# Attention and two MLPs on one core: q and k of three batches in blocks of 32 tokens, transposed by VectorE, and another order of the attention pieces

## The chip, the core and the metric

The kernel runs on one core of a Trainium2 chip. A core has TensorE (matrix products; PE in the rows, and PEld for its weight loads), VectorE (DVE), ScalarE (ACT), GpSimd (POOL), and SyncE (SP), whose queue issues most of the transfers between the chip's memory and the core's on-chip memory (SBUF). Matrix products are written to PSUM. The metric is the time of one execution in microseconds (us); lower is better.

## The reference

There are 4 batches, 8 heads, 576 tokens and 64 dimensions a head. Attention is the sum of two parts: a local one, in which a token looks at the tokens less than 4 away, and a downsampled one, in which q, k and v are averaged over groups of 4 tokens, attended to in full (144 x 144), and the result repeated 4 times. The result, 2304 tokens of 512 numbers, goes through two MLPs.

```python
q_d = q.reshape(B, H, Sd, factor, D).mean(axis=3)      # k_d, v_d alike
out_up = np.repeat(sm_attn(q_d, k_d, v_d), factor, axis=2)
mask = np.abs(pos[:, None] - pos[None, :]) < factor
scores = np.where(mask, scale * np.matmul(q, k.transpose(0, 1, 3, 2)), -1000000000.0)
# softmax, times v, plus out_up; then with x of shape (2304, 512):
h = x @ w_in;  g = h * (1.0 / (1.0 + np.exp(-1.702 * h)));  x = g @ w_out
h = x @ w_in2; g = np.where(h > 0.0, h, np.exp(np.minimum(h, 0.0)) - 1.0); y = g @ w_out2
```

## The kernel before

Attention is worked in units of one batch and two heads. Batch 0 is cut in two, four `early` units (token windows 0 to 3) and four `late` ones (windows 4 to 8), so that the first MLP can begin; the other three batches are the twelve units of `rest`. A window is 64 tokens of q against 70 of k. A unit is a list of pieces, in `pieces` (L560): the front transposes q and k (`trans`, L400: three transposes by TensorE into PSUM, a copy into `qT` or `kT` by ScalarE at L410, and after a tensor's second piece a sum over groups of four by VectorE, L416), makes the local scores (`qk`, L421: products, mask and maximum), the downsampled scores (`qk_down`, L452), and in the last piece the exponents and normalization (`exps`, L471). The back transposes the probabilities (`pdt`, `pt`) and multiplies with v (`pv_down`, `pv`). A whole unit has 8 pieces in front and 8 behind. `load_qk` (L345) brings q and k of a unit in by four transfers, six neighbouring tokens to a partition; the next unit's load is issued in the piece `k1` (L568), behind the last transposes.

The loop at L614 writes one queue: the first four front pieces of a unit, then back pieces of the unit before in turn with the rest of the front. `attend` (L639) gives out the next piece; a piece that ends a unit is held back while its block of tokens has no free buffer (L644).

The first MLP goes over the tokens in six blocks (two of 256, three of 512, one of 256), and over the hidden features in steps. A step is the products into the hidden layer (`h`, L676), their activation (ScalarE L686, VectorE L689, with a split of each number in two parts, L690 and L691), and two steps later the products out of it (`y`, L711). The loop at L903 sets all this in order: each chunk of products, half a step's `h` or half its `y`, is followed by one attention piece (three of them in the first steps), and before a block begins its attention is finished (L906). The blocks 0 and 1 are taken in turn, and during them the 32 weight tiles of the first MLP are converted by ScalarE and VectorE (`conv_w`, L144: tiles `wst1`, `ww1`, `whl1`), one part after each chunk. The hidden products have two PSUM buffers, and from that loop on all attention pieces share two (`spool`). The second MLP (`h`, L823, `o`, L872) follows, with its own weights loaded in the last block of the first.

What an engine does is in order: each has one list of instructions, made by a scheduler from the order of the code, and waits there for what an instruction needs.

Of the kernel before, what the change touches and what calls it, by code (L numbers as in the profile page):

```python
# [16 lines left out]
ALU = mybir.AluOpType  # L17
AX = mybir.AxisListType

P = 128  # L20
D = 64
S = 576
SD = 144
HALF = 72
NWIN = 9
# [41 lines left out]
def kernel(  # L67
# [20 lines left out]
    nc = tc.nc  # L88
# [16 lines left out]
    mask = cpool.tile([P, 6, KW], BF16, tag="mask", name="mask")  # L105
    nc.gpsimd.memset(mask, 0.0)
    for half in range(2):
        rows = slice(64 * half, 64 * half + 64)
        for a, e, lo in ((0, 1, -3), (1, 5, 0), (5, 6, 3)):
            m = mask[rows, a:e, :]  # L110
            for step, base, mult in ((1, -lo, -1), (-1, lo + 6, 1)):
                nc.gpsimd.affine_select(
                    out=m, in_=m, pattern=[[0, e - a], [step, KW]], compare_op=ALU.is_ge, fill=NEG,
# [193 lines left out]
    class Unit:  # L307
# [37 lines left out]
        def load_qk(self):  # L345
            self.raw = []
            b, hp = self.b, self.hp
            for nm, src in (("q", q), ("k", k)):
                r = self.t([96, 6, 2, D], f"raw{nm}")
                for j in range(2):  # L350
                    nc.sync.dma_start(
                        out=r[:, :, j, :], in_=src[b, 2 * hp + j].rearrange("(p t) d -> p t d", t=6)
                    )
                self.raw.append(r)
# [45 lines left out]
        def trans(self, which, i):  # L400
            raw = self.raw[which]
            if i == 0:
                self.qkT[which] = self.t([P, S], ("qT", "kT")[which])
            pt = self.ps([P, 3, 96], f"pt{which}{i}")
            for j in range(3):
                nc.tensor.transpose(  # L406
                    out=pt[:, j, :], in_=raw[:, 3 * i + j].rearrange("p h d -> p (h d)"),
                    identity=ident[:96, :96],
                )
            nc.scalar.activation(  # L410
                out=self.qkT[which].rearrange("c (p t) -> c t p", t=6)[:, 3 * i:3 * i + 3, :],
                in_=pt, func=AF.Copy, scale=(0.125, 1.0)[which],
            )
            if i == 1 and self.dn_from is None:
                d = self.t([P, SD], ("qd", "kd")[which])
                nc.vector.tensor_reduce(  # L416
                    out=d, in_=self.qkT[which].rearrange("c (g r) -> c g r", r=4), axis=AX.X, op=ALU.add
                )
                self.qkd[which] = d

        def qk(self, a, e):  # L421
            if a == self.w0:
                self.sl = self.t([P, self.nwin, KW], "sl", bufs=2)
                self.nm = self.t([P, NWIN], "nm", bufs=4)
            ps = self.ps([P, e - a, KW], f"qk{a}")
            m0 = 0 if a == 0 else 6 - (e - a) if e == NWIN else 1
            by_pe = self in early or self in late
            if by_pe:
                nc.tensor.matmul(
                    out=ps.rearrange("p a b -> p (a b)"), lhsT=identb,  # L430
                    rhs=mask[:, m0:m0 + e - a].rearrange("p a b -> p (a b)"),
                    start=True, stop=False, skip_group_check=True,
                )
            for w in range(a, e):
                ks = win_start(w)
                for j in range(2):
                    r = slice(64 * j, 64 * j + 64)
                    nc.tensor.matmul(  # L438
                        out=ps[r, w - a, :], lhsT=self.qkT[0][r, 64 * w:64 * w + 64],
                        rhs=self.qkT[1][r, ks:ks + KW], start=not by_pe, stop=True, skip_group_check=True,  # L440
                    )
            if by_pe:
                for w in range(a, e):
                    self.scores[w] = ps[:, w - a, :]
                scores = ps
            else:
                scores = self.sl[:, a:e]
                nc.vector.tensor_tensor(out=scores, in0=ps, in1=mask[:, m0:m0 + e - a], op=ALU.add)
            nm = self.nm[:, a:e]
            nc.vector.tensor_reduce(out=nm, in_=scores, axis=AX.X, op=ALU.max, negate=True)  # L450

        def qk_down(self, j):  # L452
            if j == 0:
                self.nmd = self.t([HALF, 4], "nmd", bufs=4)
                self.pd = self.t([HALF, 4, SD], "pd")
                self.psd = []
            r = slice(64 * j, 64 * j + 64)
            ps = self.ps([HALF, 2, SD], f"qkd{j}")
            for c in range(2):
                nc.tensor.matmul(  # L460
                    out=ps[:, c, :], lhsT=self.qkd[0][r, c * HALF:(c + 1) * HALF], rhs=self.qkd[1][r, :],
                    start=True, stop=True,
                )
            nc.vector.tensor_reduce(
                out=self.nmd[:, 2 * j:2 * j + 2], in_=ps, axis=AX.X, op=ALU.max, negate=True
            )
            if j == 1:
                nc.vector.tensor_scalar(out=self.nmd, in0=self.nmd, scalar1=1 / 16, scalar2=None, op0=ALU.mult)
            self.psd.append(ps)

        def exps(self):  # L471

# [2 lines left out]
            if down:  # L475
                for i in range(4):
                    nc.scalar.activation(
                        out=self.pd[:, i, :], in_=self.psd[i // 2][:, i % 2, :], func=AF.Exp,
                        bias=self.nmd[:, i:i + 1], scale=1 / 16, accum_out=sums[:HALF, NWIN + i:NWIN + i + 1],
                    )  # L480
            for w in range(self.w0, self.w1):
                nc.scalar.activation(
# [77 lines left out]
        def pieces(self):  # L560
# [1 line left out]
            down = self.dn_from is None  # L562
            nxt = following.get(self)
            front = []
            if down:
                self.qkT, self.qkd = [None, None], [None, None]

                def k1():  # L568
                    self.trans(1, 1)
                    if nxt is not None and self not in early:  # L570
                        nxt.load_qk()

                front += [lambda: self.trans(0, 0), lambda: self.trans(0, 1), lambda: self.trans(1, 0), k1]
            else:
                self.qkT = self.dn_from.qkT
            front += [(lambda a=a: self.qk(a, min(a + 5, self.w1))) for a in range(self.w0, self.w1, 5)]
            if down:
                front += [lambda: self.qk_down(0), lambda: (self.qk_down(1), self.exps())]
            else:
                last = front.pop()  # L580
                front.append(lambda: (last(), self.exps()))

            def pv_last(a):
                self.pv(a, self.w1)
# [29 lines left out]
    for u in units + [None]:  # L614
        front, nback = u.pieces() if u is not None else ([], [])
        pending = [(p, None) for p in back]
        if pending:
            pending[-1] = (pending[-1][0], back_of)
        lead = [(p, None) for p in front[:4]]
        queue += lead  # L620
        more = [(p, None) for p in front[4:]]
        while pending or more:
            if pending:
                queue.append(pending.pop(0))
            if more:
                queue.append(more.pop(0))
        back, back_of = nback, u
# [386 lines left out]
```

## Time and profile before

| | |
|---|---|
| median of 3 runs | 997.41 us (996.4 to 1000.46) |
| the profiled execution | 997.19 us |
| its span in the trace | 995.4 us |
| TensorE busy | 974.2 us (98%) |
| VectorE, ScalarE busy | 491.1 us (49%), 493.1 us (50%) |
| GpSimd busy | 104.1 us (10%) |
| moved by DMA | 68.05 MB, 109879 packets, 80240 of them under 512 B |

The span is what the trace covers; the execution's own time is 1.8 us longer. Shares are means over stages that are limited by different engines, so a change is priced in the stage in which it lies. Records of instructions that follow each other on one engine overlap, and what one costs is the distance from start to start. In the chain of waits that ended last, a piece's figure is the time it adds. TensorE products of float32 count twice in the trace's rows where the order of instructions counts them once; transposes count once in both.

### The profile page before, as it was taken

To read this page: it belongs to the slowest core of one execution; us is meant where nothing else is said; L and a number is where in the kernel's file an instruction comes from. 1 tells how busy PE (TensorE), PEld (TensorE's weight loads), DVE (VectorE), ACT (ScalarE), POOL (GpSimd) and SP (SyncE) were. 2 spreads that over 40 slices of the span, in tenths; PEclk is the share of its full clock that TensorE was granted. 3 is DMA by queue.
4 is the path that set the end of the run, shared out by engine and by line. 5 is a ranking of instruction groups with operands and counts; after the bars stand their busy time and mean duration, and the time that the engine had idled before them with its cause. 6 is when DMAs were issued, how large, how long until landed. Compare 5 with 4: busy or idle time off the path is not lost.

```text
span 995.4 us, 15346 instructions
## 1 busy us (share of the span) xinstructions
PE 974.2 (98%) x6124; PEld 796.2 (80%) x6124; DVE 491.1 (49%) x882; ACT 493.1 (50%) x1148; POOL 104.1 (10%) x117
## 2 busy tenths in 40 slices
PE   8988999999999999999999998999999999999998
PEld 4667899987777777778888997877888888888897
DVE  3787997554443544423223898786223222322232
ACT  4799975564444644423223566565334333433343
POOL 4355032222211200000000000000000000000000
PEclk9998999999999999999999999999999999999999
DMA  8864942242212410041003970002001100100010
GB/s 190 229 175 97 268 99 50 57 86 49 35 21 45 92 38 14 1 134 50 0 1 105 338 259 19 1 1 85 1 1 31 44 1 0 54 1 1 1 43 22
DMA packets 109879, 68.05 MB, mean 68 GB/s; under 512 B 80240, under 2 KB 99824, under 8 KB 109808
## 3 DMA queue, kind: packets, MB, share of 16 engines
q1 hardware_dynamic: 94832, 64.39, 22.6%
q0 software_dynamic: 14976, 2.69, 3.3%
q8 instruction: 48, 0.79, 0.3%
q14 instruction: 23, 0.19, 0.1%
HBM read 57.59 MB, written 9.44 MB: 67 GB/s over the span
## 4 chain that ended last, share of the span: by engine, by line
PE 82%; DVE 9%; ACT 6%; issue 1%; DMA 1%; SPq 0%; ACTq 0%; DVEq 0%
PE o L872 20%; PE h L823 19%; PE h L676 17%; PE y L711 15%; PE pv L541 2%; PE qk L438 2%; PE qkd L460 2%; PE busy L762 2%; PE ptr L515 1%; PE pt L406 1%; DVE wst2i L165 1%; DVE wst1i L165 1%; PE pvd L525 1%; DVE g1l L691 1%; DVE wst2o L165 1%
## 5 line engine op out<-in xcount | busy, mean ns | idle before, releaser
L711 PE MATMUL y<-g1h,whl1o 128*128 128x256 f32 (+1 forms) x768 | 216.0, 349 | 1.3 <-ACT g1h L690 0.7
L872 PE MATMUL o<-whl2o,g2h 128*128 128x512 f32 x576 | 181.4, 395 | 3.1 <-ACT ye L720 2.8
L676 PE MATMUL h<-xh,whl1i 128*128 128x256 f32 (+1 forms) x768 | 172.3, 348 | 2.7 <-DVE g L689 1.1
L823 PE MATMUL h<-x2h,whl2i 128*128 128x512 f32 (+1 forms) x640 | 159.0, 370 | 0.0
L711 PEld LDWEIGHTS y<-g1h,whl1o 128*128 128x128 f32 x768 | 134.9, 190 | 21.2 <-issue 4.1
L676 PEld LDWEIGHTS h<-xh,whl1i 128*128 128x128 f32 x768 | 122.3, 191 | 22.0 <-issue 2.1
L833 DVE SCALAR_TENSOR_TENSOR g<-e,h 128x512 f32<-128x512 f32 (+1 forms) x80 | 50.8, 634 | 179.8 <-ACT e L831 179.7
L823 PEld LDWEIGHTS h<-x2h,whl2i 128*128 128x128 f32 x640 | 114.3, 188 | 22.5
L711 PE MATMUL y<-g1l,whl1o 128*128 128x256 f32 (+1 forms) x384 | 130.2, 340 | 0.8 <-DVE g1l L691 0.8
L872 PEld LDWEIGHTS o<-whl2o,g2h 128*128 128x128 f32 x576 | 107.5, 189 | 28.0 <-ACT ye L720 3.2
L830 ACT ACTIVATE e<-h 128x512 f32<-128x512 f32 (+1 forms) x80 | 44.3, 554 | 161.8 <-PE h L823 161.7
L872 PE MATMUL o<-whl2o,g2l 128*128 128x512 f32 x288 | 113.0, 392 | 0.0
L365 POOL DMA_DIRECT2D vd<-in_v_dram x72 | 86.4, 1281 | 217.4 <-PE pv L541 116.2
L689 DVE SCALAR_TENSOR_TENSOR g<-g,h 128x512 f32<-128x512 f32 x72 | 49.3, 685 | 97.7 <-ACT g L686 97.7
L686 ACT ACTIVATE g<-h 128x512 f32<-128x512 f32 x72 | 43.2, 600 | 96.3 <-PE h L676 91.7
L676 PE MATMUL h<-xl,whl1i 128*128 128x256 f32 (+1 forms) x384 | 90.0, 346 | 0.0
L823 PE MATMUL h<-x2l,whl2i 128*128 128x512 f32 (+1 forms) x320 | 79.6, 370 | 0.0
L711 PEld LDWEIGHTS y<-g1l,whl1o 128*128 128x128 f32 x384 | 73.1, 191 | 7.2 <-DVE g1l L691 1.2
L840 DVE TENSOR_TENSOR g2l<-g,g2h 128x512 fp32r<-128x512 f32 (+1 forms) x80 | 51.8, 647 | 36.8 <-ACT g2h L838 21.6
L838 ACT ACTIVATE g2h<-g 128x512 fp32r<-128x512 f32 (+1 forms) x80 | 47.2, 589 | 42.9 <-DVE g L833 42.8
L676 PEld LDWEIGHTS h<-xl,whl1i 128*128 128x128 f32 x384 | 61.7, 192 | 6.5 <-issue 0.2
L690 ACT ACTIVATE g1h<-g 128x512 fp32r<-128x512 f32 x72 | 45.6, 633 | 41.2 <-DVE g L689 40.4
(107 smaller groups left out, 1203.4 us busy)
## 6 DMA issues: line engine op xcount, KB each, us to landing
wst1i<-in_moe_w_in_dram SPq DMA_DIRECT2D x16, 512.0 KB
wst1o<-in_moe_w_out_dram SPq DMA_DIRECT2D x16, 512.0 KB
wst2i<-in_moe_w_in_dram SPq DMA_DIRECT2D x16, 512.0 KB
wst2o<-in_moe_w_out_dram SPq DMA_DIRECT2D x16, 512.0 KB
rawq<-in_q_dram SPq DMA_DIRECT2D x32, 144.0 KB
rawk<-in_k_dram SPq DMA_DIRECT2D x32, 144.0 KB
ydram<-ye SPq DMA_DIRECT2D x18, 256.0 KB
out_dram<-ot SPq DMA_DIRECT2D x18, 256.0 KB
```

The source lines that it names most:

```text
L365: nc.gpsimd.dma_start(out=self.vd[:, :, j, :], in_=src, accum_op=ALU.add)
L676: nc.tensor.matmul(out=ph[:, i, :], lhsT=w_in(1, f, c, wp), rhs=xp[:, c, :], start=(n == 0), stop=(n == 3 * NK - 1),)
L686: nc.scalar.activation(out=g, in_=ph, func=AF.Tanh, scale=0.851)
L689: nc.vector.scalar_tensor_tensor(out=g, in0=g, scalar=1.0, in1=ph, op0=ALU.add, op1=ALU.mult)
L690: ins = nc.scalar.activation(out=gh, in_=g, func=AF.Copy)
L711: nc.tensor.matmul(out=yps[blk][m // nf][:, m % nf, :], lhsT=w_out(1, f, wp)[:, m, :], rhs=gp[:, i, :], start=(st == 0 and n == 0 and m % ...
L823: nc.tensor.matmul(out=ph[:, :n], lhsT=w_in(2, f, c, wp), rhs=xp[:, c, :n], start=(i == 0), stop=(i == 3 * NK - 1),)
L830: nc.scalar.activation(out=e[:, :n], in_=ph[:, :n], func=AF.Relu, scale=-1.0)
L833: urgent["dve"] = nc.vector.scalar_tensor_tensor(out=g[:, :n], in0=e[:, :n], scalar=-1.0, in1=ph[:, :n], op0=ALU.add, op1=ALU.max)
L838: nc.scalar.activation(out=gh[:, :n], in_=g[:, :n], func=AF.Copy)
L840: return lambda: nc.vector.tensor_tensor(out=gl[:, :n], in0=g[:, :n], in1=gh[:, :n].bitcast(F32), op=ALU.subtract)
L872: nc.tensor.matmul(out=ops[bi][i], lhsT=gp[:, i * P:(i + 1) * P], rhs=wo[wp], start=(f == 0 and m == 0), stop=(f == NF - 1 and m == 2),)
```

## The change

For units of `rest`, `load_qk` brings q and k in as blocks of 32 tokens by 32 dimensions: four transfers a tensor, each to 32 partitions, with 128 contiguous bytes a row in memory, where before there were two with 256. A new function `turn` has VectorE transpose all blocks of a tensor in one instruction, straight into `qT` and `kT`, then sums groups of four, and then issues the load of the unit after. It is called at the end of the last front piece of the unit before, behind that unit's exponents. The four `trans` pieces of these units are gone, with ScalarE's copies. The scale of 1/8 that the copy of q applied goes into the mask instruction and into the scale of the downsampled scores. In the queue, a unit of `rest` has its two pieces of local scores first, right behind the exponents of the unit before, then the back pieces of that unit but the last two, then its downsampled scores and exponents, and then the two back pieces left.

```diff
         def load_qk(self):
+            if self in rest:
+                for nm, src in (("q", q), ("k", k)):
+                    r = self.t([P, 6 * 2 * D], f"raw{nm}")[:, :S].rearrange("p (t d) -> p t d", d=32)
+                    for a in range(4):
+                        j, h = a // 2, a % 2
+                        nc.sync.dma_start(
+                            out=r[32 * a:32 * a + 32],
+                            in_=src[b, 2 * hp + j].rearrange("(t i) d -> i t d", i=32)[:, :, 32 * h:32 * h + 32],
+                        )
+                    self.raw.append(r)
+                return
...
+        def turn(self):
+            self.qkT, self.qkd = [None, None], [None, None]
+            for which in range(2):
+                self.qkT[which] = self.t([P, S], ("qT", "kT")[which])
+                nc.vector.transpose(out=self.qkT[which], in_=self.raw[which].rearrange("p t d -> p (t d)"))
+            for which in range(2):
+                self.sum4(which)
+            nxt = following.get(self)
+            if nxt is not None:
+                nxt.load_qk()
...
-                nc.vector.tensor_tensor(out=scores, in0=ps, in1=mask[:, m0:m0 + e - a], op=ALU.add)
+                nc.vector.scalar_tensor_tensor(
+                    out=scores, in0=ps, scalar=0.125, in1=mask[:, m0:m0 + e - a], op0=ALU.mult, op1=ALU.add
+                )
...
+            def front_last():
+                last()
+                self.exps()
+                if nxt in rest:
+                    nxt.turn()
...
-        lead = [(p, None) for p in front[:4]]
-        queue += lead
-        more = [(p, None) for p in front[4:]]
+        nlead = 2 if u in rest else 4
+        queue += [(p, None) for p in front[:nlead]]
+        more = [(p, None) for p in front[nlead:]]
+        if u in rest and len(pending) > 2:
+            queue += pending[:-2]
+            pending = pending[-2:]
+            queue += more
+            more = []
```

How this moves instructions is seen in the engines' lists. On TensorE, the third unit of batch 1 (`_1_2_`; `pt` are the transposes of q and k, `qk` its local scores, `pdt` the transposed probabilities of the unit before, `pv` the products with v, `y` and `h` the first MLP), before, from its second half of transposes on:

```order
L406 MATMUL pt_1_2_0_1939<-ident,rawk_2_0_1507 128x96 x3
L406 MATMUL pt_1_2_0_1957<-ident,rawk_2_0_1507 128x96 x3
L676 MATMUL h_1_2_1944<-xh_842,whl1i_1147 128x256 x4
L676 MATMUL h_1_2_1944<-xl_843,whl1i_1147 128x256 x4
L676 MATMUL h_1_2_1944<-xh_842,whl1i_1147 128x256 x4
L503 MATMUL pdt_1_1_0_1990<-ident,pd_1_0_1674 72x72 x4
```

and after, the same unit's scores and what follows them:

```order
L575 MATMUL pv_1_0_0_1682<-PT_0_0_1466,vw_0_0_1340 64x64 x7
L751 MATMUL y_1_1852<-g1h_1_1839,whl1o_1112 128x256
L751 MATMUL y_1_1852<-g1l_1_1840,whl1o_1112 128x256
L465 MATMUL qk_1_2_0_1731<-kT_2_0_1618,qT_2_0_1616 64x70 x10
L465 MATMUL qk_1_2_0_1766<-kT_2_0_1618,qT_2_0_1616 64x70 x8
L751 MATMUL y_1_1852<-g1h_1_1839,whl1o_1112 128x256
L537 MATMUL pdt_1_1_0_1800<-ident,pd_1_0_1577 72x72 x4
```

The transposes of q and k are gone; both pieces of scores stand together, and the transposed probabilities follow behind one product, where twelve stood between two pieces before.

On VectorE, the place where the last weight tile of the first MLP is done (`whl1o`), before:

```order
L182 TENSOR_TENSOR whl1o_2327<-ww1o_2148,whl1o_2327 128x512
L171 SCALAR_TENSOR_TENSOR ww1o_2285<-ww1o_2285,wst1o_1699 128x512
L689 SCALAR_TENSOR_TENSOR g_0_7_2320<-g_0_7_2320,h_0_7_2272 128x512
L182 TENSOR_TENSOR whl1o_2351<-ww1o_2285,whl1o_2351 128x512
L691 TENSOR_TENSOR g1l_7_2323<-g_0_7_2320,g1h_7_2322 128x512
L416 TENSOR_REDUCE qd_3_0_2358<-qT_3_0_2332 128x144
L416 TENSOR_REDUCE kd_3_0_2398<-kT_3_0_2373 128x144
```

and after, where the downsampled probabilities of the fourth unit of batch 1 (`pd_3`) are normalized ahead of it and the transposes of the first unit of batch 2 lie about it:

```order
L527 TENSOR_TENSOR pd_3_0_2314<-pd_3_0_2314,sumset 72x576
L527 TENSOR_TENSOR sl_3_0_2098<-sl_3_0_2098,sumset 128x630
L729 SCALAR_TENSOR_TENSOR g_0_7_2447<-g_0_7_2447,h_0_7_2399 128x512
L441 STREAM_TRANSPOSE qT_0_0_2353<-rawq_0_0_2006 128x576
L182 TENSOR_TENSOR whl1o_2487<-ww1o_2412,whl1o_2487 128x512
L431 TENSOR_REDUCE qd_0_0_2357<-qT_0_0_2353 128x144
L731 TENSOR_TENSOR g1l_7_2450<-g_0_7_2447,g1h_7_2449 128x512
```

By the end of the conversions VectorE has done a whole unit's scores more than before, and a fifth unit's transposes have begun. From the activation `g_0_1` to this last `whl1` instruction it has 169 instructions before and 193 after; from there to the activation `g_1_7`, the last of block 1, 195 and 236.

On SP's queue, the load of q and k of the fourth unit of batch 1, before:

```order
L391 DMA vw_1_0_1852<-in_v_dram 70x64
L351 DMA rawq_3_0_1964<-in_q_dram 96x6x64 x2
L351 DMA rawk_3_0_1967<-in_k_dram 96x6x64 x2
L363 DMA vd_1_0_2235<-in_v_dram 72x2x64 x2
L391 DMA vw_2_0_2301<-in_v_dram 70x64
```

and after:

```order
L375 DMA vd_0_0_1548<-in_v_dram 72x2x64 x2
L354 DMA rawq_3_0_1624<-in_q_dram 32x18x32 x4
L354 DMA rawk_3_0_1629<-in_k_dram 32x18x32 x4
L136 DMA wst1i_1680<-in_moe_w_in_dram 128x4x128
L403 DMA vw_1_0_1694<-in_v_dram 70x64
```

Four transfers of 96x6 rows have become eight of 32x18, and the load now stands ahead of the v of that batch's second unit (`vw_1`), where it stood behind it; a weight tile (`wst1i`) and that v wait behind the eight.

## Rows read from the trace of the kernel before

**Rows 1.** The page: span, busy time by engine, TensorE and its clock in 40 slices.
```profile
span 995.4 us, 15346 instructions
...
PE 974.2 (98%) x6124; PEld 796.2 (80%) x6124; DVE 491.1 (49%) x882; ACT 493.1 (50%) x1148; POOL 104.1 (10%) x117
...
PE   8988999999999999999999998999999999999998
...
PEclk9998999999999999999999999999999999999999
```

**Rows 2.** Busy time of each engine by stage; clock, DMA share and GB/s last.
```profile
core 0: us, PE busy (x) PEld busy (x) DVE busy (x) ACT busy (x) POOL busy (x), PEclk, DMA share, GB/s
...
69.00:110.00 41.00, 36.84 (x332) 32.73 (x332) 34.36 (x69) 38.39 (x85) 16.74 (x14) 0.92 0.71 153
110.00:163.00 53.00, 50.97 (x515) 47.08 (x514) 52.26 (x101) 40.85 (x111) 12.22 (x10) 1.00 0.52 129
69.00:163.00 94.00, 87.81 (x844) 79.81 (x844) 86.61 (x169) 79.24 (x195) 28.97 (x24) 0.96 0.60 140
69.00:194.00 125.00, 118.81 (x1148) 109.01 (x1148) 99.97 (x195) 93.56 (x239) 35.48 (x29) 0.97 0.52 119
205.00:433.00 228.00, 227.76 (x1602) 173.09 (x1601) 100.93 (x198) 107.71 (x321) 33.94 (x30) 1.00 0.22 41
433.00:540.00 107.00, 107.00 (x500) 87.94 (x500) 30.64 (x49) 29.08 (x52) 0.00 (x0) 1.00 0.13 45
540.00:600.00 60.00, 56.10 (x427) 53.87 (x427) 49.72 (x79) 36.57 (x63) 0.00 (x0) 1.00 0.84 285
```

**Rows 3.** The chain that ended last, in order of time: start, us, what.
```profile
237.63 0.25 PE pt L406 x3
237.88 1.43 PE h L676 x6
239.31 0.25 PE pt L406 x3
...
505.77 2.72 PE y L711 x12
```

**Rows 4.** Line 406 from 85 to 440 us: duration ns min/median/max, first and last start.
```profile
L406 PE MATMUL pt<-ident,rawq x72: 243/244/417, 91.1 to 394.4; 96*128 96x96 f32 x72
...
L406 PE MATMUL pt<-ident,rawk x72: 243/245/368, 95.6 to 397.7; 96*128 96x96 f32 x72
```

**Rows 5.** Groups of VectorE, 69 to 163 us: busy us, mean ns | idle before.
```profile
L448 DVE TENSOR_TENSOR sl<-qk,mask 128x350 f32<-128x350 f32 (+1 forms) x6 | 3.0, 508 | 0.0
...
L416 DVE TENSOR_REDUCE qd<-qT 128x144 f32<-128x576 f32 x3 | 2.3, 753 | 0.1
```

**Rows 6.** Groups of the whole span: ScalarE's copy of transposed q.
```profile
L410 ACT ACTIVATE qT<-pt 128x288 f32<-128x288 f32 x26 | 17.9, 720 | 30.7 <-PE pt L406 30.6
```

**Rows 7.** TensorE's longest waits from 69 to 205 us: in total, times, longest.
```profile
PE pt L406 <- ACT qT L410: 1.7, 1, 1.7
PE pdt L503 <- ACT kT L410: 1.2, 2, 0.9
```

**Rows 8.** SP's issues of q and k in order of time: start, us.
```profile
37.62 4.99 SPq L351 DMA_DIRECT2D rawk<-in_k_dram  x2
...
97.90 1.44 SPq L351 DMA_DIRECT2D rawq<-in_q_dram  x2
99.44 3.69 SPq L351 DMA_DIRECT2D rawk<-in_k_dram  x2
...
239.59 2.41 SPq L351 DMA_DIRECT2D rawq<-in_q_dram  x2
242.92 1.24 SPq L351 DMA_DIRECT2D rawk<-in_k_dram  x2
```

**Rows 9.** Stretches as rows 2; queue 1's packets, MB, share, 239-250 and 112-118 us.
```profile
246.00:247.00 1.00, 1.00 (x21) 0.91 (x22) 0.27 (x1) 0.60 (x1) 0.00 (x0) 1.00 0.25 51
247.00:248.00 1.00, 1.00 (x6) 0.79 (x5) 0.97 (x3) 0.55 (x1) 0.00 (x0) 1.00 0.00 0
...
q1 hardware_dynamic: 2944, 0.73, 30.6%
...
q1 hardware_dynamic: 1573, 2.10, 101.7%
```

**Rows 10.** VectorE in order of time: the last activation of block 1.
```profile
194.02 0.69 DVE L689 SCALAR_TENSOR_TENSOR g<-g,h 128x512 f32<-128x512 f32 x1 [1.79 <-ACT g L686]
```

More of the change, by code (lines that the diff above doesn't have):

```diff
@@ L414, in trans, with sum4 @@
             if i == 1 and self.dn_from is None:
[L415 to L419, printed above, removed]
+                self.sum4(which)
+        def sum4(self, which):
+            d = self.t([P, SD], ("qd", "kd")[which])
+            nc.vector.tensor_reduce(
+                out=d, in_=self.qkT[which].rearrange("c (g r) -> c g r", r=4), axis=AX.X, op=ALU.add
+            )
+            self.qkd[which] = d
+        def turn(self):
[4 more added lines that the diff above has]
+            for which in range(2):
+                self.sum4(which)
+            nxt = following.get(self)
+            if nxt is not None:
+                nxt.load_qk()
         def qk(self, a, e):
@@ L447, in qk @@
                 scores = self.sl[:, a:e]
-                nc.vector.tensor_tensor(out=scores, in0=ps, in1=mask[:, m0:m0 + e - a], op=ALU.add)
+                nc.vector.scalar_tensor_tensor(
+                    out=scores, in0=ps, scalar=0.125, in1=mask[:, m0:m0 + e - a], op0=ALU.mult, op1=ALU.add
+                )
             nm = self.nm[:, a:e]
@@ L467, in qk_down, with scale_down @@
             if j == 1:
-                nc.vector.tensor_scalar(out=self.nmd, in0=self.nmd, scalar1=1 / 16, scalar2=None, op0=ALU.mult)
+                nc.vector.tensor_scalar(
+                    out=self.nmd, in0=self.nmd, scalar1=self.scale_down(), scalar2=None, op0=ALU.mult
+                )
             self.psd.append(ps)
+        def scale_down(self):
+            return 1 / 128 if self in rest else 1 / 16
         def exps(self):
@@ L478, in exps @@
                         out=self.pd[:, i, :], in_=self.psd[i // 2][:, i % 2, :], func=AF.Exp,
-                        bias=self.nmd[:, i:i + 1], scale=1 / 16, accum_out=sums[:HALF, NWIN + i:NWIN + i + 1],
+                        bias=self.nmd[:, i:i + 1], scale=self.scale_down(), accum_out=sums[:HALF, NWIN + i:NWIN + i + 1],
                     )
@@ L564, in pieces @@
             front = []
-            if down:
+            if down and self not in rest:
                 self.qkT, self.qkd = [None, None], [None, None]
[L568 to L574, printed above, removed]
+                front += [(lambda w=w, i=i: self.trans(w, i)) for w in range(2) for i in range(2)]
+            elif not down:
                 self.qkT = self.dn_from.qkT
@@ L577, in pieces @@
             if down:
[L578 to L581, printed above, removed]
+                front += [lambda: self.qk_down(0), lambda: self.qk_down(1)]
+            last = front.pop()
+            def front_last():
[3 more added lines that the diff above has]
+                    nxt.turn()
+            front.append(front_last)
             def pv_last(a):
```

## The prediction, made before the changed kernel ran

> **What bounds the kernel now.** I read the page first: TensorE is busy for 974.2 of 995.4 us [rows 1], so the question is whether that is one limit or several. The table by stage answers it [rows 2]. From 205 to 433 us, where attention pieces lie between the products of the first MLP, TensorE is busy 227.76 of 228 us and VectorE 100.93: there every column given to TensorE counts, and nothing else does. From 433 to 540 us it is busy all the time without attention. Before 205 us it is different. From 69 to 163 us the kernel also converts the weights of the first MLP; VectorE is busy 86.61 of 94 us, and from 110 to 163 us 52.26 of 53, while TensorE still reaches 87.81 of 94. Two engines are nearly full there, and the change loads one and relieves the other. From 600 us on the change touches nothing.
>
> **What it removes from TensorE.** A unit of the three batches has four pieces of three transposes; 72 + 72 matmul records from 91 to 398 us [rows 4] are twelve units, 48 pieces. What a piece costs is read from the chain [rows 3], not from the 244 ns of one record, since the records overlap: from one piece to the next 239.31 - 237.63 = 1.68 us pass with six products between them. Twelve products without a piece take 2.72 us, so six take 1.36, and a piece costs 0.32 us, 0.25 of its own and 0.07 in the products behind it. 48 x 0.32 = 15.4 us less work for TensorE. ScalarE loses 48 copies of 0.72 us [rows 6], most of them where it isn't waited for. Two waits of TensorE on these copies, 1.7 and 1.2 us [rows 7], lose their cause; I count nothing for them, since in the new order other waits stand at the same places (below).
>
> **What it adds to VectorE.** Two transposes of 128x576 float32 a unit. No row shows one. The nearest is the reduction that reads the same 576 elements a partition, 753 ns [rows 5]; I take that. As the upper end I take what ScalarE needs to carry the same tile over, two copies of 0.72, 1.44 us [rows 6]; as the lower end the 0.69 us of the 512-element operations about it [rows 10]. Scale and mask in one instruction replaces the mask addition, 508 ns [rows 5], one for one; the nearest row of the new form, 0.69 us for 512 elements [rows 10], is no dearer by the element. I take zero for it, and at most 24 x 0.1 = 2.4 us, all hidden after 205 us. The scales move into instructions that exist.
> The Trainium skill, page "VectorE: DVE Perf Modes", section "The three transpose paths", gives 311 ns for a 128x128 bf16 transpose on VectorE. Scaled by columns, my estimate from that page is 1.40 us for one of ours; with it the sum below would be some 7 us worse, about what the 1.44 us of the copies gives. No run here shows a transpose on VectorE yet.
>
> **What it moves.** A unit has 12 pieces instead of 16, and one piece is given out per half chunk of products, so attention runs ahead. The order of instructions, put beside the trace, prices that. Up to the last hidden product of block 1, whose activation VectorE reached at 194.02 us [rows 10], VectorE ran 195 instructions from 69 us on in 99.97 us [rows 2], 0.513 us each. The changed program has 236 there: 12 transposes, and nearly one more unit of masks, maxima, normalizations and downsampled sums, with the first split of block 2. 41 x 0.513 = 21.0 us more, 121.0 of the same 125 us. The last conversion lies behind 193 instructions instead of 169 (98.9 us where 94 were). TensorE's own work up to that product comes out equal, priced by the chain's pieces: 16 transposing pieces less (5.1 us), and about 6 us of scores and products of a further unit drawn forward. So nothing is won before 194 us, and the 15.4 us are won behind it, where TensorE is full and VectorE less than half.
> What does it cost before 194 us? VectorE's waits from 69 to 110 us, 41 - 34.36 = 6.6 us [rows 2], belong to ScalarE (38.39 of 41 us busy), which the extra exponents keep as full as before. 121.0 + 6.6 = 127.6, against 125: 2.6 us late. The new order also lets scores, transposes of probabilities and their copies follow each other with one to five products between, at five places before the third block's middle; the scores take both PSUM buffers and the next transposes wait for VectorE. I give these 0.3 us each, 1.5 us. Together 4 us; the bounds are 0 (all in VectorE's gaps) and, at 1.44 us a transpose, 12 x 0.69 = 8.3 us more, 12 us.
>
> **Loads.** q and k of a unit become eight transfers instead of four, with 128-byte rows instead of 256. In the quiet stage four take 239.59 to 244.16 us to issue [rows 8] and have landed by about 246.3 us [rows 9]: 6.7 us. Eight would take some 13. A row costs 16 x 11 us x 0.306 / 2944 = 18.3 ns of one DMA engine [rows 9], so 4608 of them, at most at that price each, 5.3 us of all sixteen, against 2.6: 12 x 2.6 = 32 us of transfer in a stretch whose queues are busy 0.22 to 0.71 of the time. The next load is issued as soon as a unit's transposes are done, a unit ahead (some 20 to 30 us), so I count zero; at worst a wait of some 4 us where two turns lie closest, at the start of block 2. SP's queue is in order: behind the q and k loads stand weights and v, which are used over 10 us later.
> Against the change speaks the Trainium skill, "DMA: Bandwidth & Descriptors", section "Specifications": transfers under 512 B fall short of line rate, with a read-modify-write. The trace agrees for 256 B: 0.73 MB in 30.6% of 11 us is 13.5 GB/s an engine, against 21.5 for the weights' larger rows (2.10 MB in 101.7% of 6 us) [rows 9]; it bears on the sum only if the loads come late.
>
> **Sum.** The profiled execution took 997.19 us (span 995.4), 0.2 under the median of the runs, 997.41. 997.2 - 15.4 + 4 = 985.8; I forecast 986 us, and 981 to 991 for this case alone.
>
> **Rivals.**
> 1. A transpose takes twice what I took. VectorE then is 8.3 us later in the conversion stage, and its order pushes the activations back: 986 + 8.3 = 994. For it: nothing in the trace has this form, and ScalarE's copies of the same tile cost 1.44 us. Against: every VectorE row of about that size lies near 0.7 us [rows 5, 10].
> 2. The scores do not follow "at once" with profit: with two PSUM buffers, TensorE waits at each unit's transposes of probabilities until VectorE has masked the scores, twice 0.5 us [rows 5] in twelve units, 12 us: 986 + 12 - 1.5 = 996. For it: in the changed order the first of them stands one product behind the scores. Against: that holds for five units; the later ones have six products (1.36 us) between.
> 3. Slower. VectorE's transposes wait for their load, and VectorE is in order: the activation of the hidden products stands behind them, and with two buffers for these TensorE stops soon after. Where the DMA queues are full, two transfers took 4.99 us to issue [rows 8]; eight would take 20 and land about 23 us after the turn. From 20 us on, the spacing of the turns in the early stage, the rest is a wait. At 4.3 us in each of four units there it costs 17 us: 1003. For it: DMA is 0.71 busy from 69 to 110 us. Against: at 97.90 us, with the weights' transfers about it, the four took 5.2 us to issue [rows 8], so eight some 10; and the first unit's load is issued 25 us or more before its use.
> 4. All of it comes back: VectorE's extra fits into its gaps and the two waits on the copies go as well: 997.2 - 15.4 - 2.9 = 979.
>
> **Chances.** My forecast 0.55; rival 1 0.13, rival 2 0.10, rival 3 0.10, rival 4 0.12. About 0.5% (5 us) is what a measurement of this kernel can tell from no change. Under 992.2 us lie the forecast, rival 4 and a few hundredths of rivals 1 and 2: 0.71. Rivals 1 and 2 and a little of the forecast's upper edge are no change, 0.19; rival 3 with some tail is slower, 0.10. The range of 979 to 997 us leaves out rival 3 and the edge of rival 4.
>
> **What would show it.** Right: no matmul of the transposing line after 100 us; VectorE transposes near 0.75 us; the last hidden product of block 1 activated between 194 and 199 us after the start; attention over some 40 us before 433 us; the stage of heavy DMA at 540 us beginning 11 us earlier, and from there to the end the trace merely shifted. Wrong: transposes over 1.2 us, TensorE idle for over 12 us from 69 to 205 us, or VectorE waiting for the q or k load for over 1 us a unit. If that last product comes earlier than 190 us, I have overpriced VectorE's crowding; if it comes on time but the gain behind it is under 12 us, the piece's price of 0.32 us is wrong.

## The result, and the profile after: 13 us slower

The changed kernel takes 1010.23 us, median of 4 runs (1009.46 to 1011.15); the kernel before took 997.28 beside it (996.4 to 1000.46). The ratio is 1.0122, 95% interval 1.0102 to 1.0143. The prediction said 986, faster; it was wrong in sign, and the time lies outside its range.

The page of the changed kernel's profiled execution (1011.15 us), to be held against [rows 1]:

```profile
span 1009.4 us, 15093 instructions
...
PE 971.8 (96%) x5980; PEld 796.1 (79%) x5980; DVE 508.1 (50%) x906; ACT 461.9 (46%) x1100; POOL 103.3 (10%) x117
...
PE   8987799899999999999999998999999999999998
...
PEclk9996799899999999999999999999999999999999
```

TensorE has 144 instructions less, but its busy time fell by 2.4 us only, and in the fourth slice the granted clock fell to 0.6. Where the time went is seen in the stretches (columns as in [rows 2]):

```profile
69.00:110.00 41.00, 30.72 (x243) 27.19 (x241) 29.03 (x55) 30.64 (x70) 17.23 (x15) 0.77 0.53 112
110.00:163.00 53.00, 48.44 (x444) 43.62 (x444) 45.67 (x88) 33.26 (x98) 8.03 (x7) 0.92 0.61 153
69.00:163.00 94.00, 79.16 (x684) 70.81 (x683) 74.70 (x143) 63.90 (x166) 25.27 (x22) 0.85 0.58 135
205.00:433.00 228.00, 225.29 (x1684) 175.01 (x1684) 115.19 (x225) 92.22 (x315) 33.96 (x30) 0.99 0.30 60
540.00:600.00 60.00, 58.90 (x423) 55.71 (x422) 39.65 (x64) 29.30 (x52) 0.00 (x0) 1.00 0.71 246
```

From 69 to 163 us TensorE is 8.65 us less busy than before, and so are VectorE (74.70 after 86.61) and ScalarE (63.90 after 79.24). No engine is full: each waits for another. A second loss stands in the same rows: while the lower clock is granted, a busy TensorE does less. Like products show it in the changed kernel (start, us, instruction, idle before): four ahead of an idle time and four behind it, and eight at a granted clock of 0.50 (195 to 200 us) and at 1.00 (215 to 220 us):

```profile
190.05 0.74 PE L716 MATMUL h<-xh,whl1i 128*128 128x256 f32 x4 [0.31 <-DVE whl1i L182]
194.41 1.22 PE L716 MATMUL h<-xh,whl1i 128*128 128x256 f32 x4 [3.62 <-DVE g L729]
...
196.29 1.91 PE L716 MATMUL h<-xh,whl1i 128*128 128x256 f32 x8
197.99 1.05 PE L716 MATMUL h<-xl,whl1i 128*128 128x256 f32 x4
...
217.69 1.12 PE L716 MATMUL h<-xh,whl1i 128*128 128x256 f32 x8
218.65 0.64 PE L716 MATMUL h<-xl,whl1i 128*128 128x256 f32 x4
```

From start to start the eight take 1.70 us at the lower clock and 0.96 at the higher, 1.8 times as long.

To compare kernels I count *lost TensorE time*: the length of a window, less its busy time multiplied by the granted clock, summed over windows of 5 us from the span's start to 300 us, behind which hardly any is lost for some 200 us. (It prices the lower clock at twice the time, a little more than these rows show.) Before 18.1 us, after 46.5: 28.4 us more. Less the 15.4 us of work removed that is 13.0. It can be held against the place where the first MLP ends, the first copy of its last block out of PSUM, before and after:

```profile
539.81 0.58 ACT L720 ACTIVATE ye<-y 128x512 f32<-128x512 f32 x1
553.32 0.58 ACT L760 ACTIVATE ye<-y 128x512 f32<-128x512 f32 x1
```

That is 13.5 us later, so up to there the ledger closes; the spans differ by 14.0. By stretch, before and after: 80 to 100 us 4.3 and 11.7; 100 to 130 us 1.3 and 10.0; 130 to 190 us 1.0 and 2.4; 190 to 200 us 0.4 and 6.4; 200 to 250 us 0.2 and 4.5. From 65 to 300 us idle time alone is 7.0 and 22.6 us, work lost at the lower clock 3.2 and 16.1.

One point parts the loss from the gain, the start of the last products into the hidden layer of block 1, before and after:

```profile
192.65 0.65 PE L676 MATMUL h<-xh,whl1i 128*128 128x256 f32 x4
219.13 0.64 PE L716 MATMUL h<-xh,whl1i 128*128 128x256 f32 x4
```

They come 26.5 us later. From there to the end of the first MLP the changed kernel takes 13.0 us less (334.2 after 347.2).

TensorE's waits from 69 to 205 us (in total, times, longest), against [rows 7]:

```profile
PE y L751 <- ACT whl1o L178: 6.0, 2, 5.0
PE h L716 <- ACT whl1i L178: 4.3, 4, 2.4
PE h L716 <- DVE g L729: 3.6, 1, 3.6
...
PE qk L465 <- DVE kT L441: 0.3, 1, 0.3
```

The longest of these waits are for converted weights and for an activation, hardly any for the transposes. The longest wait, 4.96 us until 85.62, can be followed back in VectorE's order:

```profile
75.91 0.77 DVE L441 STREAM_TRANSPOSE kT<-rawk 128x576 f32<-128x576 f32 x1
80.00 0.69 DVE L729 SCALAR_TENSOR_TENSOR g<-g,h 128x512 f32<-128x512 f32 x1 [3.32 <-ACT g L726]
80.61 0.74 DVE L431 TENSOR_REDUCE kd<-kT 128x144 f32<-128x576 f32 x1
81.39 0.69 DVE L731 TENSOR_TENSOR g1l<-g,g1h 128x512 fp32r<-128x512 f32 x1
82.00 0.81 DVE L165 TENSOR_SCALAR wst1o<-wst1o 128x512 uint16<-128x512 uint16 x1
84.21 0.69 DVE L171 SCALAR_TENSOR_TENSOR ww1o<-ww1o,wst1o 128x512 int32<-128x512 int32 x1 [1.40 <-ACT wst1o L168]
```

The shift of a w_out tile (line 165) stands behind the activation of step (0,2) and starts at 82.00. The same place before:

```profile
75.18 1.35 DVE L165 TENSOR_SCALAR wst1o<-wst1o 128x512 uint16<-128x512 uint16 x2
77.36 0.69 DVE L171 SCALAR_TENSOR_TENSOR ww1o<-ww1o,wst1o 128x512 int32<-128x512 int32 x1 [0.83 <-ACT wst1o L168]
78.78 0.69 DVE L689 SCALAR_TENSOR_TENSOR g<-g,h 128x512 f32<-128x512 f32 x1 [0.73 <-ACT g L686]
```

There the shifts ran at 75.18, ahead of the activation; now VectorE idles 3.32 us with the activation at the head of its list, and they stand behind it. The conversions from there to the product all start late, and each waits for the one before it on the other engine. The tiles' transfers had been issued at the same time in both kernels (55.74 and 55.65 us).

### The profile page after: what moved, and what is told of

The parts are those of the page before. It is cut to its first block, busy times and chain, and to the rows that moved or that the text cites. A ratio compares the mean times of both kernels' runs of the same rounds, so it can differ in the third digit from the quotient of the medians.

```text
span 1009.4 us, 15093 instructions
## 1 busy us (share of the span) xinstructions
PE 971.8 (96%) x5980; PEld 796.1 (79%) x5980; DVE 508.1 (50%) x906; ACT 461.9 (46%) x1100; POOL 103.3 (10%) x117
## 4 chain that ended last, share of the span: by engine, by line
PE 80%; DVE 11%; ACT 7%; issue 1%; DMA 1%; SPq 0%; DVEq 0%; ACTq 0%
PE o L912 20%; PE h L863 19%; PE h L716 17%; PE y L751 16%; PE pv L575 2%; PE qk L465 2%; PE busy L802 2%; PE ptr L549 1%; PE qkd L489 1%; DVE wst2i L165 1%; ACT pd L511 1%; ACT wst1o L168 1%; DVE g L729 1%; PE pdt L537 1%; ACT wst1i L168 1%
## 5 line engine op out<-in xcount | busy, mean ns | idle before, releaser
L751 PEld LDWEIGHTS y<-g1h,whl1o 128*128 128x128 f32 x768 | 137.9, 195 | 28.6 <-ACT whl1o L178 6.5
L716 PEld LDWEIGHTS h<-xh,whl1i 128*128 128x128 f32 x768 | 126.5, 196 | 30.7 <-ACT whl1i L178 5.3
```

The lines of the kernel that those rows point to most:

```text
L716: nc.tensor.matmul(out=ph[:, i, :], lhsT=w_in(1, f, c, wp), rhs=xp[:, c, :], start=(n == 0), stop=(n == 3 * NK - 1),)
L751: nc.tensor.matmul(out=yps[blk][m // nf][:, m % nf, :], lhsT=w_out(1, f, wp)[:, m, :], rhs=gp[:, i, :], start=(st == 0 and n == 0 and m % ...
```

## The experiments

Each expectation weighs theories against each other. 'Order': the place that the new queue gives scores and exponents; 'VectorE': its added work; 'pace': a unit has 12 pieces instead of 16 and they are given out as fast as before, so that attention presses in among the conversions; 'list': the shifts of w_out stand behind an activation in VectorE's list; 'moved up': the transposes, moved up that list, displace conversions; 'filler': the removed transposes filled time in which TensorE now waits.

Lost time is that up to 300 us; before has 18.1, the changed kernel 46.5. It belongs to the profiled execution alone, whose time stands beside it and can lie some us off the median. Each ratio is to runs of the kernel before taken beside it (medians 997.04 to 997.78). The unit is turned on TensorE ("PE") or VectorE ("DVE"). The code shown is shortened.

| run | what it is | median us | ratio to before, 95% | profiled us | lost us |
|---|---|---|---|---|---|
| e1 | DVE, old order, 16 pieces | 1000.47 | 1.0014 to 1.0043 | 1000.29 | 38.4 |
| e2 | DVE at the exponents, dealt in turn, 12 pieces | 1007.27 | 1.0076 to 1.0122 | 1006.00 | 41.0 |
| e3 | PE, new rule of the queue | 1001.15 | 1.0022 to 1.0060 | 1005.29 | 27.0 |
| e4 | PE at the exponents, new rule | 1004.68 | 1.0053 to 1.0107 | 1004.54 | 23.7 |
| e5 | before, 128-byte loads | 998.94 | 0.9992 to 1.0019 | 1000.36 | 20.8 |
| e6 | e1, transposes held in place | 1003.27 | 1.0029 to 1.0057 | 1000.77 | 34.5 |
| e7 | e1, first load later | 996.02 | 0.9971 to 1.0008 | 998.56 | 33.6 |
| e8 | DVE for two batches | 992.27 | 0.9907 to 0.9959 | 994.73 | 25.1 |
| e9 | e8, turned at the exponents | 1001.57 | 1.0026 to 1.0058 | 999.93 | 26.7 |
| e10 | e9 with the new rule | 998.46 | 0.9994 to 1.0029 | 1001.09 | 29.2 |
| e11 | changed, first load later | 1004.60 | 1.0056 to 1.0093 | 1003.71 | 37.8 |
| e12 | changed, 16 pieces | 1006.50 | 1.0073 to 1.0107 | 1007.21 | 43.9 |
| e13 | changed, dummy PE transposes | 1018.13 | 1.0172 to 1.0227 | 1017.51 | 35.0 |
| e14 | before, dummy DVE transposes | 1004.76 | 1.0039 to 1.0080 | 1005.35 | 26.4 |
| e15 | DVE from the sixth unit | 993.89 | 0.9930 to 0.9970 | 991.61 | 21.7 |
| e16 | DVE for one batch | 993.23 | 0.9940 to 0.9977 | 991.76 | 17.1 |

**Engine and order taken apart: e1 to e4.** In e1 the four lead pieces are VectorE's and the queue is the old one:

```
 front += [lambda: self.turn(w, i) ...]    # turn q, sum q, turn k, sum k
-nlead = 2 if u in rest else 4 ...         # and the block that moves `more`
+queue += front[:4]; more = front[4:]
```

> q and k turned by VectorE as in the changed kernel, but as four pieces at the head of a unit (turn q, sum q, turn k, sum k), and the queue of pieces in the order of the kernel before: only the engine of the transposes changes. Theory 'order' (the loss comes from the place that the new queue gives the scores and exponents among the weight conversions): 981 to 988 us, the 15.4 us of TensorE work won. Theory 'VectorE' (21 us more on VectorE in the conversion stage is too much): 1005 to 1012 us. Theory 'pace' (12 pieces for a unit at an unchanged three pieces for a chunk press more attention between the conversions): 981 to 988, since a unit has 16 pieces again.

It came out between: 3.4 us slower than before. With the engine changed (and with it the form of the loads and the place of the scale) and the old order, 15.4 us were to be won and 3.4 were lost: 18.8 us have gone. No theory had that. The stall is at the same place, 80 to 90 us, before and in e1:

```profile
80.00:90.00 10.00, 9.01 (x92) 7.69 (x91) 9.14 (x21) 9.87 (x23) 7.08 (x6) 1.00 0.50 92
80.00:90.00 10.00, 5.30 (x35) 4.22 (x35) 6.96 (x10) 8.11 (x10) 7.31 (x7) 0.53 0.27 23
```

e2 keeps the transposes behind the exponents and deals out the scores in turn (`nlead = 0`, the block that moves `more` taken out):

> The changed kernel with its transposes behind the exponents and 12 pieces for a unit, but the scores dealt out in turn with the pieces of the unit before, as in the kernel before. Theory 'order': 981 to 990 us. Theories 'VectorE' and 'pace': 1005 us or more.

1007.3: theory "order" alone falls. e3 puts the new rule of the queue into the kernel before (`nlead = 6`, and the block that moves `more`):

> The kernel before with its TensorE transposes (16 pieces for a unit), and the new rule for the queue alone: a unit's first scores directly behind its transposes, the rest of the scores and the exponents before the last two pieces of the unit before. Theory 'order': 1008 to 1015 us. Theories 'VectorE' and 'pace': 995 to 1000.

4.1 us slower (2.2 to 6.0 by the interval), above the one range and below the other: the order costs something, far from all. Its lost time is that of the slowest of its nine runs. e4 issues TensorE's four pieces in `turn`, with the changed kernel's queue:

> The changed kernel's queue, 12 pieces for a unit, with TensorE's transposes and ScalarE's copies issued all four at the place of the VectorE transposes, and the loads of the kernel before. Theory 'order' and theory 'pace': 1010 to 1025 us (the loss of 29 us on top of the 997, less what the old transposes fill). Theory 'VectorE': 996 to 1003.

7.6 us over before, 1.7 above the range of 'VectorE', but 5.5 under the changed kernel, whose TensorE has 15.4 us less to do. With TensorE's transposes, only 23.7 us are lost. Before, e1, e4 and the changed kernel make a table of two by two: the exchange of the engine costs 3.4 us in the old order (e1) and 5.3 in the new one, where it was to win 15.4; the new order, pace and place of the transposes cost 7.6 us with TensorE (e4) and 9.5 with VectorE (times less those of before).

**Loads, moving up, and the place of the conversions: e5 to e7.** e5 is the kernel before with each q and k transfer split:

```
-nc.sync.dma_start(out=r[:, :, j, :], in_=tokens)
+for c in halves: nc.sync.dma_start(out=r[:, :, j, c], in_=tokens[:, :, c])
```

> The kernel before with TensorE's transposes and its queue; only the loads of q and k of the last three batches are split into 8 transfers of 128-byte rows (4608 rows a unit, as the changed kernel has them). Theory 'loads' (these rows hold back the weights behind them, on the chip): 1002 us or more. Theory 'list' (the loss comes from where VectorE's list has the conversions of w_out; here its list has the shift of the third pair of w_out tiles ahead of the hidden product of step (0,2), as in the kernel before) and theory 'VectorE': 996 to 1000.

No difference that can be told (at most 1.9 us by the interval): 128-byte rows are not the cause. e6 holds each transpose behind the VectorE instruction issued ahead of it (`with tc.issue_after(latest(nc.vector.engine)):` about the body of `turn`):

> VectorE transposes in the old order (as e1), but each is held behind the VectorE instruction that is issued ahead of it in the program, so that none moves up VectorE's list into the conversions 30 us before it is wanted. The shift of w_out still stands behind the hidden product of step (0,2). Theory 'moved up' (transposes that have moved up the list displace the conversions): 981 to 990 us. Theory 'list' (what counts is the conversion behind the hidden product): some 7 us of the 20 lost in e1 stay, 990 to 1001. Theory 'VectorE': 998 to 1003.

1003.3, no better than e1, and 80 to 90 us still loses 6.8 us: that transposes move up the list is not it; the shift of w_out stood behind the activation here too. e7 moves `rest[0].load_qk()` behind `wt1.need("i", 1)`, which puts the shifts ahead of the activation again:

> VectorE transposes in the old order (as e1), with the load of the first unit's q and k issued behind the first conversions instead of ahead of them: VectorE's list then has the shifts of both w_out tiles before the hidden product of step (0,2), the first transpose still ahead of it. Theory 'list': the 6.3 us that TensorE lost more from 80 to 90 us come back: 990 to 996 us. Theory 'VectorE': 998 to 1003, the wait comes at another place. Theory 'moved up': 998 to 1003.

996.0, 4.5 us under e1. TensorE in that stretch is at full clock, though it still loses 3.5 us, so that 3.8 of the 6.3 us come back there:

```profile
80.00:90.00 10.00, 6.48 (x71) 5.44 (x70) 7.07 (x12) 5.62 (x7) 6.64 (x6) 1.00 0.38 44
```

So the place of the conversions in the list is worth 4 to 5 us. But e7 still loses 12 us from 190 to 240; its longest wait there is for the transposes themselves:

```profile
PE qk L463 <- DVE kT L439: 3.3, 1, 3.3
PE h L709 <- DVE g L722: 1.5, 1, 1.5
```

There the first block of 512 tokens begins and the queue is emptied until it is ready. Before, TensorE ran its transposing pieces between (209.22 to 211.9 us); now TensorE has nothing until VectorE has turned q and k.

**Only where TensorE is full: e8 to e10.** e8 keeps TensorE's transposes and the old loads for the first batch:

```
-if self in rest:
+if self in rest[4:]:        # so for the block loads, VectorE's turn and the scale; held as in e6
```

> TensorE transposes and the old loads for the first of the three batches, VectorE transposes (held in their place as in e6) and block loads for the last two, whose units come behind the weight conversions; old order of the queue. 32 of the 48 transposing pieces go, 32 x 0.32 = 10.2 us of TensorE work. All theories that put the loss into the conversion stage (list, moved up, VectorE): 985 to 990 us. Theory 'VectorE also later' (e1 lost 11 us of TensorE time from 200 to 240 us too, behind the conversions): 992 to 1000.

992.3, 5.5 us faster than before (4.1 to 9.3 by the interval) and the lowest median measured, at the edge of 'VectorE also later'; of 10.2 us about half is kept, and 4 us go from 220 to 230, the wait on VectorE's activation again (DVE g, 1.5 us, then products at the lower clock). e9 turns a unit behind the exponents of the one before:

> As e8 (TensorE transposes for the first of the three batches, VectorE for the last two), but a VectorE-transposed unit is turned behind the exponents of the unit before it, as in the changed kernel, and its scores are dealt out in turn with the older pieces. In e8 TensorE lost 4 us more than before from 220 to 230 us, where a block needs the attention finished and a unit's four transposing pieces give TensorE nothing to do. Theory 'empty lead' (this is the wait): 986 to 990 us. Otherwise as e8, 990 to 995.

My "empty lead" failed: 1001.6, above both ranges. TensorE then waits for other links of the same chain, exponents and x, at this start of a block and at the next, where it loses another 5.4 us. Its longest waits from 340 to 362 us:

```profile
PE ptr L552 <- ACT pd L514: 1.6, 1, 1.6
PE qkd L492 <- ACT PT L556: 0.7, 1, 0.7
```

e10 adds the new rule for these two batches:

> As e9, with the changed kernel's rule for the queue for the last two batches alone: the scores directly behind the exponents of the unit before. Theory 'the new order costs only among the conversions': as e9, within 2 us. Theory 'the new order costs wherever it stands': 4 us or more above e9 (e3 was 4 us slower than before by the order alone).

998.5, 3 us better than e9 instead of 4 worse: the rule's cost in e3 belongs to its place among the conversions, or to chance in the order; I can't tell which. The traces don't show the 3 us: the profiled execution of e10 is 1.2 us slower than that of e9, and at the second of these block starts it loses 8.7 us where e9 loses 5.4.

**The changed kernel mended in one point: e11, e12.** e11 has the edit of e7:

> The changed kernel, with the load of the first unit's q and k issued behind the first conversions (the edit of e7). VectorE's list has the shifts of w_out ahead of the hidden product of step (0,2) again. Theory 'list': as e1 to e7, 4 to 8 us come back: 1002 to 1006. Theory 'pace' or 'order' alone: 1008 to 1012.

5.6 us come back, as the list theory says; the loss from 80 to 100 us fell from 11.7 to 6.2. In e7 and e11 the first unit's transposes come later too (in e11 at 79.83 and 82.48 us, 69.97 and 75.91 without the edit); but in e6 they start at 84.17 and 86.01, and with the shift behind the activation the loss stays. e12 puts four empty pieces (`front += [lambda: None] * 4`) ahead of a unit's scores:

> The changed kernel, with four empty pieces at the head of each unit of the last three batches, so that a unit has 16 pieces again at three pieces for a chunk; the rule of the queue, the transposes and the loads stay. Theory 'pace': 1000 to 1005 us. Theory 'list' and theory 'order': 1008 to 1012.

3.7 us come back, less than the 5 to 10 that "pace" asks and more than the others allow, though only 2.6 us of the lost time went; the pace has a part at most.

**What the rest is: e13, e14.** e13 puts TensorE's work back, at the place of VectorE's transposes, and nothing else:

```
+nc.tensor.transpose(out=pt[:, j, :], in_=raw[which][...], identity=ident)  # 12 a unit, never read
```

> The changed kernel, with 12 TensorE transposes added for each unit right behind VectorE's (the columns and count of the ones that the change removed; nothing reads their results): 15.4 us of TensorE work is put back, nothing is taken from VectorE or ScalarE but ScalarE's copies stay away. Theory 'filler' (the removed transposes ran where TensorE now waits, so they are worth little there): 1008 to 1016 us, at most 6 above the changed kernel. Theory 'work' (each transpose removed is 0.32 us won, the loss comes from elsewhere): 1022 to 1027.

Between the two: 7.9 us slower for 15.4 us of work. Half of it fell into time that was lost anyway; lost time fell from 46.5 to 35.0 us. From 65 to 300 us idle time went from 22.6 to 18.6 us and the loss at the lower clock from 16.1 to 8.4, so most of what the filler gave back is clock:

```profile
69.00:300.00 231.00, 212.67 (x1902) 181.38 (x1901) 164.08 (x314) 125.67 (x378) 67.60 (x58) 0.96 0.46 92
```

against the changed kernel's

```profile
69.00:300.00 231.00, 208.69 (x1804) 178.04 (x1803) 163.66 (x314) 126.29 (x385) 65.82 (x57) 0.92 0.47 91
```

e14 adds VectorE's transposes to the kernel before, into the tile of the scores just ahead of them:

```
+nc.vector.transpose(out=flat, in_=self.qkT[which])    # twice a unit
```

> The kernel before, with two VectorE transposes (128x576, 0.77 us each) added for each of the 12 units just ahead of its first scores (their results are overwritten by the scores); TensorE's transposes, loads and queue stay. Theory 'VectorE' (its added 18.4 us are what makes the others late): 1004 us or more. Theory 'list and filler': 996 to 1001.

It costs 7.0 us (3.9 to 8.0 by the interval), most of it up to 120 us (TensorE had lost 6.7 us more than before by then). So VectorE's added work does cost in the conversion stage, against theories "list" and "filler". It isn't the sum of the work: only four of the 24 transposes, 3.1 us, stand before 130 us, and the twenty behind them cost almost nothing. Whether the four cost by their own time or by the order in which the conversions then stand is not told apart.

**Where the work is won: e15, e16.** e8's edit with `rest[5:]` and `rest[8:]`:

> As e8, with VectorE transposes from the sixth of the 12 units on, not from the fifth: the unit at the start of the first block of 512 tokens, where e8 lost 4 us more than before from 220 to 230 us, keeps TensorE's. Theory 'filler' (TensorE's transposes cover that wait): 986 to 991 us, 28 x 0.32 = 9.0 us won and 0 to 2 lost. Otherwise 992 to 996.

> As e8, with VectorE transposes for the last batch alone (4 units, 16 x 0.32 = 5.1 us of TensorE work): all theories 990 to 994 us where no block start falls into them; 994 to 998 if each stage with attention loses as much as it gains.

e15 didn't reach 986 to 991: 993.9. Its profiled execution lost 3.4 us less than that of e8 and was 3.1 us faster, but the medians of the two can't be told apart. e16 does what the prediction expected of the whole change. It takes away 5.1 us of TensorE work, loses no more than before, and is 4.5 us faster; before and e16:

```profile
69.00:300.00 231.00, 224.21 (x1955) 190.79 (x1955) 151.46 (x297) 147.34 (x406) 62.33 (x53) 0.99 0.42 88
69.00:300.00 231.00, 223.52 (x1948) 189.76 (x1947) 151.24 (x297) 146.77 (x404) 63.87 (x53) 0.99 0.42 87
```

## Why the prediction was wrong, point by point

- *48 pieces of 0.32 us, 15.4 us of TensorE work.* It fits: the ledger closes with it, and e16, all of whose 16 pieces stood behind 299 us, gains 4.5 us (2.3 to 6.0) of 5.1.
- *A VectorE transpose at 0.753 us, up to 1.44.* Right; the line of the changed kernel (min/median/max ns, and who waited for it):

```profile
L441 DVE STREAM_TRANSPOSE qT<-rawq x12: 765/768/818, 70.0 to 361.2; 128x576 f32<-128x576 f32 x12
L441 DVE STREAM_TRANSPOSE kT<-rawk x12: 764/767/820, 75.9 to 362.2; 128x576 f32<-128x576 f32 x12
...
  PE qk L465: 0.3, 1
```

  From the Trainium skill ("VectorE: DVE Perf Modes", "The three transpose paths") the prediction had estimated 1.40 us; the measurement decides, and it is about half of that. (At 1.40 us the twelve transposes would have added 7.8 us, not some 7.) Rival 1 is out.
- *Loads counted zero.* Right: no idle time stands before these transposes, and e5 is the same as before. Rival 3, 1003, came nearest to the time, by a mechanism that did not happen.
- *"What does it cost before 194 us? ... 121.0 + 6.6 = 127.6, against 125: 2.6 us late ... Together 4 us; the bounds are 0 ... 12 us."* This step failed. The activation of the last hidden product of block 1 started on VectorE at 230.64 us (194.02 before [rows 10], forecast 194 to 199), and up to that product TensorE lost 24.8 us more than before (34.4 after 9.6 from 69 us on), not 4. VectorE's instructions and their sum were as forecast; its waits were not. Before and after, from the second activation to this one (the column of VectorE is the third):

```profile
69.43:194.02 124.59, 118.40 (x1146) 108.60 (x1145) 99.55 (x196) 93.15 (x239) 35.48 (x29) 0.97 0.52 118
69.37:230.64 161.27, 139.78 (x1273) 125.15 (x1272) 123.98 (x236) 94.49 (x264) 45.46 (x39) 0.89 0.50 104
...
230.64 0.67 DVE L729 SCALAR_TENSOR_TENSOR g<-g,h 128x512 f32<-128x512 f32 x1
```

  VectorE is busy for 124.0 us (forecast 121.0) with 236 instructions, but it idles for 37.3. I let 6.6 us of waits stay and the added work run in the rest of its 25.0 us of idle time; instead the waits grew. From 69 to 163 us VectorE ran fewer instructions than before (143 after 169) and was busy for 74.70 of 94 us: its list has a new order, and in this order it waits. Nor did the bound of 12 us hold, since it is made of VectorE's durations too. "TensorE's own work up to that product comes out equal" was right: busy time multiplied by the granted clock is 115.1 us before and 116.2 after, from 69 us to the end of that product.
- *The clock had no term.* 16.1 - 3.2 = 12.9 us of the 28.4 are work at the lower clock, most of it behind waits of 2 to 5 us. No run took it away by itself; e13, which only gives TensorE more to do, halved it.
- *"... the 15.4 us are won behind it, where TensorE is full"* (behind the last hidden product of block 1). In the main: 13.0 us were won behind it. Some is lost again at the start of the block of 512 tokens, where TensorE is not full without its transposes: 4.3 us from 220 to 250 us, nothing before.
- Rival 2: TensorE waited 1.2 us for masked scores in all of attention (`qk <- DVE sl`), not 12. Rival 4, that all fits into gaps, is out.
- Of its own tests, "TensorE idle for over 12 us from 69 to 205 us" came true: 10.28 + 4.56 + 4.77 = 19.6 us (6.6 before). Attention ended 18 us earlier (last product at 419.5 us, 437.2 before), not 40, and the first tile of the second MLP is converted at 565.0 us, 14 later than before (550.8), not 11 earlier; from there the trace is shifted.

What the 28.4 us are made of, as far as runs show: the place of the w_out conversions some 5 us (e7, e11); VectorE's added work in the old order 7 (e14); half of the removed work, 7.5, not to be won while TensorE waits (e13, at one place for the pieces); the rule of the queue 4 with TensorE's transposes (e3), the pace up to 4 (e12). They overlap and were not shown to add. That the loss comes from the first of the three batches is shown more plainly: e8 differs from e6 in that batch alone and is 11 us faster. Why the conversions move in the list is open: the block loads or VectorE's transposes do it (e1, e6), 128-byte rows alone do not (e5).

## What to carry to other kernels

Price work that leaves a full engine only in stretches where it is full to the last wait; where engines feed each other in turn, such work also fills waits, and taking it away uncovers them. A sum of busy times bounds nothing there: compare the order of the conversions and activations at each place that feeds the bottleneck, and add a term for the clock: here 15.6 us more of idle time came with 12.9 us more at the lower clock. A change that gains in one stage and loses in another is worth making in the first stage alone, as e8, e15 and e16 did.

## What was not expected of the hardware

- VectorE turned 128x576 float32 in 0.768 us, hardly more than a reduction over the same data (0.74).
- After single waits of 3.62 and 4.96 us TensorE ran at its lower granted level (0.5 of the higher; 1.2 of 2.4 GHz): four 128x256 products took 1.22 us after the idle time of 3.62 us, 0.74 shortly ahead of it; eight took 1.70 us from start to start, 0.96 at the higher level.
- 4608 rows of 128 bytes a unit in place of 256 cost nothing measurable (e5, 0.9992 to 1.0019).
